# Rows of h for six of twelve chunks taken from PE through PSUM in place of DMA, with new scheduling targets

## The chip, the cores and the metric

The kernel runs on one core of a Trainium2 chip. A core has five engines that run side by side: PE (TensorE, matrix products into PSUM), DVE (VectorE), ACT (ScalarE), POOL (GpSimd) and SP, which here issues transfers. SBUF is the working memory of 128 partitions; PSUM, which PE writes and DVE and ACT read, has eight banks. Sixteen DMA engines carry out transfers. The metric is device time in microseconds (us); lower is better.

## The reference

A windowed attention feeds a gated feed-forward layer with a convolution along the sequence. The batch is 8, there are 8 heads of 64, the sequence is 576; the window is 32 to either side; d_model is 512, d_ff 1024, and the convolution has three taps.

```
scores = scale * (q @ k.T)            # masked outside the window, then softmax
x      = softmax(scores) @ v          # heads joined: (8, 576, 512)
h      = relu(x @ w_in)               # (8, 576, 1024)
conv   = sum_k conv_w[k] * h shifted by k - 1 along the sequence
out    = (h * sigmoid(conv)) @ w_out  # (8, 576, 512) float32
```

## The kernel before

**Tiling.** Attention runs by batch and by pair of heads: load q and k, cast to bf16, transpose on PE, scores on PE, exp on ACT, mask on DVE, values on PE, and the division by the row sums on DVE (`xn`). `xn` is transposed on PE into `xT`. The feed-forward part runs over twelve chunks of 384 rows of the sequence, three chunks for two batches (`ffn`, L942). For each of eight blocks m of 128 features, `first` (L747) multiplies by `w_in`, and a relu with factor 0.5 on ACT or DVE writes `hT`. Then come the convolution and the gate for four blocks at a time (`gates`, L856), and `second` (L912) multiplies the product `gT` by `w_out`. Chunk 1 is done in two halves of 192 columns; chunks 1, 4, 7 and 10 straddle two batches.

**The convolution and the turned rows.** The three taps are done on PE with 32x32 diagonal matrices (`diag_w`). To keep all sixteen 32x32 tiles of the array at work, rows 32r to 32r+31 of block m are written to the output partitions that begin at 32((r + m) mod 4):

```
to = 32 * ((r + m) % 4)
tensor.matmul(bank(ps, i)[to:to + 32, 0:n], diag_w[32 * r:32 * r + 32, kk, m, :], taps(m, kk, 32 * r, 32 * r + 32), ...)
```

So the convolution of block m comes out with its rows turned by 32 times (m mod 4). ACT takes the tanh of it (two instructions of two banks, into `tn`), and DVE forms (tanh + 1) times h, which needs h turned by the same amount; w_out's rows are loaded turned alike. For the first block of four the turn is nil and DVE reads h from `hT`. For the other three, `moves` (L822) issues DMAs on SP that copy h, with its rows turned, from `hT` into `gT` (two DMAs for each turn, since it wraps around), and the product then overwrites `gT` in place. The product is one instruction for block 0, one for block 1, and one for blocks 2 and 3 together.

**The order.** The kernel does not leave its order to a compiler. Each step is handed to a planner (`Order.add`, L42) with the engines that may do it, an estimate of its duration, what it reads and writes, the number of PSUM banks that it opens, and a target time. `Order.run` (L76) walks through a model of the engines: whenever an engine is free, it takes the ready step with the smallest target. The order that comes out is the order of the instructions in the program, and it is kept. Targets come from a formula (`PARAMS`) and are replaced by the entries of `TIMES`, one list for each kind of step. The names are `qk` and `v` for loads, `mv` for moves, `ph` for first products, `rl` for relus, `cv` for convolutions, `th` for tanh, `pr` for gate products, `py` for second products, and so on. The planner also sets dummy matmuls (`warm`) where it expects PE to be idle in the first 95 us.

All transfers but five go through SP's one queue in that order: loads of q, k, v and the weights, moves of h, and stores of the result. An instruction that waits there holds up what stands behind it.

The constant `GE`, the number of chunks whose rows are moved by DVE or ACT, is 0 here, so all twelve chunks use DMAs.

Of the kernel before, what the change touches and what calls it, by code (L numbers as in the profile page):

```python
# [16 lines left out]
GE = 0  # L17

# [196 lines left out]
def kernel(  # L215
# [98 lines left out]
    def two(kind):  # L314

        return kind[0], kind[1], "port"
# [391 lines left out]
    def x_turned(b, c, n):  # L708

        t, d = pair_t[b * NP + NP - 1]  # L710
        t = t + Q["XT"] * d + 0.1 * c + (Q["B0"] if b == 0 and c else 0.0)
# [110 lines left out]
    def moves(c, qds, part, t):  # L822
        kind, halves, n, taps, gate = views(c, part)
        for s_ in range(1, 4):
# [15 lines left out]
            if c < GE:  # L840
                continue
# [14 lines left out]
    def gates(c, qd, part, t, late):  # L856
# [27 lines left out]
        for m0, count, us in ((0, 1, (0,)), (1, 1, (0,)), (2, 2, (1,))):  # L884
            m = 4 * qd + m0
            ii = [("h", kind, m, p_) for p_ in halves] if m0 == 0 else [
                ("gm", c % 3, m + x, p_, to) for x in range(count) for p_ in halves for to in range(0, 128, 32)]

            def product(e, m=m, m0=m0, count=count):
                if count > 1:  # L890
                    vector.scalar_tensor_tensor(
                        out=gate(m, count=count), in0=tn[:, m0:m0 + count, 0:n], scalar=1.0,
                        in1=gate(m, count=count), op0=ALU.add, op1=ALU.mult)
                else:
                    vector.scalar_tensor_tensor(
                        out=gate(m), in0=tn[:, m0, 0:n].rearrange("p (i x) -> p i x", x=HW),
                        scalar=1.0, in1=gate(m) if m0 else taps(m, 1), op0=ALU.add, op1=ALU.mult)

            o.add("pr", {"DVE": two(dve(n * count))}, product, late,
                  reads=[("tn", tn_i, u) for u in us] + ii,  # L900
# [66 lines left out]
    for b in range(B):  # L967
# [48 lines left out]
    "wic": [0.16, 15.86, 10.72, -5.27, 20.24, 27.55, 66.33, 50.26],  # L1016
# [113 lines left out]
```

## Time and profile before

| | |
|---|---|
| time, median of three runs | 243.39 us (242.74 to 246.04) |
| time of the profiled execution | 244.45 us |
| its span, first to last instruction | 242.5 us |
| granted PE clock, mean | 0.965 |
| busy share of PE, DVE, ACT, POOL | 89%, 69%, 73%, 20% |
| moved by DMA | 49.63 MB in 67420 packets |

The profile is one execution, seen by the hardware profiler. Busy time is the time in which at least one instruction of the engine was under way. In rows of groups stand the line (L295, a helper that records every operation), the engine, the operation, what it writes and reads with the shapes, the count, and then busy us and the mean ns of one instruction, and the idle time of the engine ahead of it with what ended it. The matmuls overlap, so that their mean is longer than busy time divided by count. The granted clock is the share of full speed that PE was allowed. A chain of waits follows the work that ended last back to the start.

### The profile page before, as it was taken

The page shows a single profiled execution, that of the slowest core. Times are in us where ns is not written, and L with a number is a line of the kernel's source. Part 1 is how long each engine was busy: PE and PEld are TensorE (multiplying, and loading weights), DVE is VectorE, ACT ScalarE, POOL GpSimd, SP SyncE. Part 2 cuts the span into 40 slices and gives each one's busy share as a digit, 9 for nine tenths or more (in the row PEclk, how much of TensorE's full clock was granted, in tenths as well). Part 3 has the DMA queues.
Part 4 walks back from the last instruction along what each step waited for, and adds up shares of the span by engine and source line. Part 5 has one row for each costly group of instructions (what it writes and reads, how often), then busy time and mean ns, then how long its engine had stood idle before and what let it go on. Part 6 is the DMA issues. An engine that isn't in the chain of part 4 may idle for free.

```text
span 242.5 us, 9363 instructions
## 1 busy us (share of the span) xinstructions
PE 215.5 (89%) x4004; PEld 130.6 (54%) x4035; DVE 168.2 (69%) x313; ACT 176.8 (73%) x308; POOL 47.8 (20%) x60
## 2 busy tenths in 40 slices
PE   2788797579999859989999999999999999999993
PEld 1546684355655447556556455565556556554441
DVE  7264967965149796999689788989787697217530
ACT  2658788777699858867985898789495958567541
POOL 4414243211355340110433121112000000000000
PEclk9999999759999985999999999999999999999999
DMA  6999999989999898959979999955125033125334
GB/s 151 232 296 277 379 187 252 240 208 357 310 229 300 228 327 221 288 113 283 256 194 254 255 221 272 277 150 182 40 76 174 3 132 100 39 74 181 111 132 182
DMA packets 67420, 49.63 MB, mean 205 GB/s; under 512 B 46364, under 2 KB 52532, under 8 KB 67380
## 3 DMA queue, kind: packets, MB, share of 16 engines
q1 hardware_dynamic: 67024, 48.44, 74.1%
q10 hardware_dynamic: 356, 0.60, 1.1%
q8 instruction: 31, 0.51, 1.0%
q14 instruction: 9, 0.07, 0.1%
HBM read 32.52 MB, written 9.44 MB: 173 GB/s over the span
## 4 chain that ended last, share of the span: by engine, by line
PE 61%; DMA 21%; ACT 6%; issue 4%; DVE 3%; SPq 3%; POOL 1%; ACTq 0%; POOLq 0%
PE pst L295 61%; DMA vst<-in_v_dram 6%; DMA qst<-in_q_dram 5%; DMA kst<-in_k_dram 4%; DMA wst<-in_moe_w_out_dram 3%; SPq L295 3%; DMA out_dram<-wst 2%; ACT attn L295 2%; DVE xn L295 1%; ACT kT L295 1%; ACT qb L295 1%; ACT wst L295 1%; ACT tn L295 1%; ACT hT L295 1%; DVE xT L295 1%
## 5 line engine op out<-in xcount | busy, mean ns | idle before, releaser
L295 PE MATMUL pst<-xT,w_in_sb 128*128 128x385 bf16 (+3 forms) x448 | 72.5, 307 | 1.0 <-DVE xT L295 0.7
L295 PE MATMUL pst<-w_out_sb,gT 128*128 128x512 bf16 x261 | 63.7, 379 | 3.0 <-issue 0.9
L295 PEld LDWEIGHTS <-w_in_sb 128*128 128x128 bf16 x448 | 39.7, 98 | 23.5 <-issue 3.4
L295 PEld LDWEIGHTS <-gT 128*128 128x128 bf16 x288 | 27.2, 98 | 30.5 <-issue 1.3
L295 ACT ACTIVATE attn<-pst 128x640 bf16<-128x640 f32 (+1 forms) x64 | 39.2, 665 | 3.8 <-PE pst L295 3.7
L295 ACT ACTIVATE tn<-pst 128x768 f32<-128x768 f32 (+1 forms) x52 | 37.8, 760 | 5.8 <-PE pst L295 5.4
L295 DVE SCALAR_TENSOR_TENSOR gT<-tn,gT 128x384 bf16<-128x384 f32 (+2 forms) x52 | 37.3, 737 | 4.3 <-ACT tn L295 2.5
L295 ACT ACTIVATE hT<-pst 128x385 bf16<-128x385 f32 (+3 forms) x74 | 33.7, 460 | 9.1 <-PE pst L295 8.2
L295 ACT COPY wst<-pst 128x512 f32<-128x512 f32 x34 | 19.9, 585 | 24.5 <-PE pst L295 24.1
L295 DVE TENSOR_SCALAR hT<-pst 128x385 bf16<-128x385 f32 (+3 forms) x38 | 18.0, 478 | 21.9 <-PE pst L295 11.7
L295 DVE TENSOR_TENSOR attn<-attn,mask 128x1152 bf16<-128x1152 bf16 (+2 forms) x36 | 27.0, 764 | 7.2 <-ACT attn L295 6.9
L295 DVE TENSOR_TENSOR xn<-pst,rec 128x640 bf16<-128x640 f32 (+2 forms) x36 | 25.8, 737 | 0.4
L295 POOL CAST ve<-vst 128x512 bf16<-128x512 f32 x21 | 15.0, 722 | 37.9 <-DMA vst<-in_v_dram 29.4
L295 PE MATMUL pst<-hT,diag_w 32*32 32x384 bf16 (+1 forms) x1248 | 21.5, 321 | 1.1 <-ACT hT L295 0.6
L295 POOL CAST qb<-qst 128x1152 bf16<-128x1152 f32 (+1 forms) x13 | 14.3, 1100 | 39.4 <-DMA qst<-in_q_dram 23.1
L295 PE MATMUL pst<-qT,kT 64*128 64x64 bf16 x576 | 17.1, 197 | 4.2 <-ACT attn L295 1.7
L295 PEld LDWEIGHTS <-kT 64*128 64x128 bf16 x576 | 12.0, 98 | 13.0 <-issue 9.7
L295 PEld LDWEIGHTS <-attn 128*64 128x64 bf16 x640 | 13.1, 115 | 10.0 <-issue 5.2
L295 PEld LDWEIGHTS <-diag_w 32*32 32x32 bf16 x1248 | 12.5, 88 | 11.0 <-issue 8.1
L295 PE MATMUL pst<-ve,attn 128*64 128x65 bf16 x384 | 15.4, 200 | 3.1 <-ACT attn L295 1.5
L295 POOL CAST kb<-kst 128x1152 bf16<-128x1152 f32 (+1 forms) x10 | 11.0, 1099 | 22.5 <-DMA kst<-in_k_dram 19.5
L295 DVE SCALAR_TENSOR_TENSOR gT<-tn,hT 128x384 bf16<-128x384 f32 (+1 forms) x26 | 14.2, 545 | 1.5 <-ACT tn L295 1.5
(47 smaller groups left out, 207.1 us busy)
## 6 DMA issues: line engine op xcount, KB each, us to landing
out_dram<-wst SPq DMA_DIRECT2D x11, 768.0 KB, 4.0
qst<-in_q_dram SPq DMA_DIRECT2D x14, 576.0 KB, 7.8
kst<-in_k_dram SPq DMA_DIRECT2D x14, 576.0 KB, 6.9
vst<-in_v_dram SPq DMA_DIRECT2D x24, 256.0 KB, 6.3
vst<-in_v_dram SPq DMA_DIRECT2D x16, 192.0 KB, 8.3
wst<-in_moe_w_in_dram SPq DMA_DIRECT2D x2, 1024.0 KB, 7.5
gT<-hT SPq DMA_DIRECT2D x14, 144.0 KB, 3.7
gT<-hT SPq DMA_DIRECT2D x34, 48.0 KB, 4.0
```

The source lines that it names most:

```text
L295: return lambda *args, **kwargs: fixed(do(*args, **kwargs))
```

## The change

For chunks 0 to 5 (`GH` is 6) the moves are left out. In their place stands a step `hr` on PE behind each convolution: twelve 32x32 matmuls with an identity (`ident32`, which was there before) write h of blocks 1 to 3, turned, into three PSUM banks. DVE's products for these blocks read h from there instead of from `gT`. The product of blocks 2 and 3 becomes two instructions. For the planner, products that read PSUM do not use the port that DVE and POOL share. Chunks 6 to 11 are as before. Each target in `TIMES` is another number, there are 14 targets for `hr`, and `mv` has 27 in place of 51. A branch in `x_turned` that transposes by DMA is added for batches from `XB`, which is 9, on.

```
+GH = 6
+XB = 9
+XL = 1800.0
...
     def x_turned(b, c, n):
         t, d = pair_t[b * NP + NP - 1]
+        if b >= XB:
+            for i in range(n):
+                o.add("xd", {"SP": dma(512, 25, 1, XL)}, lambda e, i=i: sync.dma_start(
...
+                          transpose=True),
...
+            return
...
-            if c < GE:
+            if c < max(GE, GH):
                 continue
...
+        hp = Banks(3) if c < GH else None
+        if hp:
+            def again(e):
+                for m0 in (1, 2, 3):
+                    for r in range(4):
+                        to = 32 * ((r + m0) % 4)
+                        tensor.matmul(
+                            bank(hp, m0 - 1)[to:to + 32, 0:n], ident32[32 * r:32 * r + 32, :],
+                            taps(4 * qd + m0, 1, 32 * r, 32 * r + 32), start=True, stop=True,
+                        )
+            o.add("hr", {"PE": pe(n / 2.4 + 60.0, "conv")}, again, late - 0.5,
+                  reads=[("pc", c, qd, part)], writes=[("hr", c, qd, part)], opens=hp,
+                  claims=[("g", c % 3, m, p_) for m in ms[1:] for p_ in halves],
+                  sub=qd + 2 * int(c == 1 and part == 0))
-        for m0, count, us in ((0, 1, (0,)), (1, 1, (0,)), (2, 2, (1,))):
+        for m0, count, us in (
+            ((0, 1, (0,)), (1, 1, (0,)), (2, 1, (1,)), (3, 1, (1,))) if hp
+            else ((0, 1, (0,)), (1, 1, (0,)), (2, 2, (1,)))
+        ):
...
-                        scalar=1.0, in1=gate(m) if m0 else taps(m, 1), op0=ALU.add, op1=ALU.mult)
+                        scalar=1.0, in1=(
+                            taps(m, 1) if not m0 else gate(m) if not hp
+                            else bank(hp, m0 - 1)[:, 0:n].rearrange("p (i x) -> p i x", x=HW)
+                        ), op0=ALU.add, op1=ALU.mult)
-            o.add("pr", {"DVE": two(dve(n * count))}, product, late,
-                  reads=[("tn", tn_i, u) for u in us] + ii,
+            o.add("pr", {"DVE": dve(n * count) if hp and m0 else two(dve(n * count))}, product, late,
+                  reads=[("tn", tn_i, u) for u in us] + ii, ps=[hp] if hp and m0 else [],
...
 TIMES = {
...
+    "hr": [51.56, 44.36, 55.05, 40.86, 66.04, 57.58, 88.82, 87.48, 113.53, 111.1, 98.45, 122.43, 128.37,
+        103.87],
...
```

More of the change, by code (lines that the diff above doesn't have):

```diff
@@ L710, in x_turned @@
         t, d = pair_t[b * NP + NP - 1]
+        if b >= XB:
+            for i in range(n):
+                o.add("xd", {"SP": dma(512, 25, 1, XL)},
+                      lambda e, i=i: sync.dma_start(
+                          xT_pp[b // 2 % 2][:, :, b % 2, 128 * (c + i):min(S, 128 * (c + i) + 128)],
+                          xn_pp[b % 2][0:min(128, S - 128 * (c + i)), c + i, :, :].rearrange("p h d -> p (h d)"),
+                          transpose=True),
+                      t + Q["XT"] * d + 0.1 * (c + i), reads=[("xn", b % 2, i_, p_) for i_ in range(NP) for p_ in (0, 1)],
+                      writes=[("xT", b // 2 % 2, b % 2, c + i)], sub=c + i)
+            return
         t = t + Q["XT"] * d + 0.1 * c + (Q["B0"] if b == 0 and c else 0.0)
@@ L883, in gates @@
                   sub=qd + 2 * int(c == 1 and part == 0))
-        for m0, count, us in ((0, 1, (0,)), (1, 1, (0,)), (2, 2, (1,))):
+        hp = Banks(3) if c < GH else None
[16 more added lines that the diff above has]
+        ):
             m = 4 * qd + m0
-            ii = [("h", kind, m, p_) for p_ in halves] if m0 == 0 else [
+            ii = [("h", kind, m, p_) for p_ in halves] if m0 == 0 else [("hr", c, qd, part)] if hp else [
                 ("gm", c % 3, m + x, p_, to) for x in range(count) for p_ in halves for to in range(0, 128, 32)]
@@ L999 @@
 TIMES = {
[16 rows of a table removed]
-    "wic": [0.16, 15.86, 10.72, -5.27, 20.24, 27.55, 66.33, 50.26],
[36 rows of a table removed]
-    "woc": [92.89, 108.38, 80.47, 26.38, 74.95, 60.09, 73.65, 29.52],
[44 rows of a table removed]
[16 rows of a table added]
+    "wic": [9.77, -0.55, 23.61, 66.31, 22.41, 46.77, 25.62, 17.63],
[36 rows of a table added]
+    "woc": [40.32, 59.04, 39.76, 27.86, 36.19, 43.45, 41.37, 49.63],
[47 rows of a table added]
 }
```

193 rows, old and new, of the table TIMES are left out of this document.

## The prediction

> **What bounds the kernel now.** I read the page first: busy tenths, clock, DMA row, and the chain that ended last.
>
> ```profile
> PE   2788797579999859989999999999999999999993
> ...
> PEclk9999999759999985999999999999999999999999
> DMA  6999999989999898959979999955125033125334
> ...
> q1 hardware_dynamic: 67024, 48.44, 74.1%
> ...
> PE 61%; DMA 21%; ACT 6%; issue 4%; DVE 3%; SPq 3%; POOL 1%; ACTq 0%; POOLq 0%
> ```
>
> A slice is 242.5 / 40 = 6.06 us. The DMA engines are full for 26 slices, to about 160 us, and then nearly idle; PE has its holes and its lowered clock in the first 16. So there are two stages. The chain in order of time (start, us, what) shows the border, for after this piece it is PE almost alone:
>
> ```profile
> 149.60 3.48 PE pst L295 x95
> ```
>
> The windows view, cut there, gives the stages in numbers (stretch, length, then busy us of PE, PEld, DVE, ACT, POOL, the granted clock, the DMA share, GB/s); the fourth row is the same view for the dummy matmuls alone, which keep PE awake and compute nothing:
>
> ```profile
> 20.00:150.00 130.00, 115.06 (x2352) 74.41 (x2366) 99.84 (x177) 103.78 (x183) 38.02 (x41) 0.93 0.98 258
> 100.00:160.00 60.00, 57.43 (x1109) 34.05 (x1119) 52.97 (x87) 48.67 (x84) 12.94 (x13) 1.00 0.94 235
> 150.00:242.50 92.50, 87.66 (x1480) 48.81 (x1488) 57.64 (x98) 62.73 (x110) 3.22 (x4) 1.00 0.43 125
> ```
> ```profile
> 20.00:150.00 130.00, 4.41 (x9) 1.26 (x12) 0.00 (x0) 0.00 (x0) 0.93 0.98 258
> ```
>
> Stage one, 20 to 150: DMA 98% busy, PE 115.06 - 4.41 = 110.65 us of real work in 130. Stage two: PE 87.66 of 92.5, nothing else near its limit. Who waits in stage one, and for what, shows the waits view (us in total, times, longest), first for all engines from 20 to 150, then for the SP queue from 0 to 150:
>
> ```profile
> POOL ve L295 <- DMA vst<-in_v_dram: 22.3, 11, 7.2
> POOL kb L295 <- DMA kst<-in_k_dram: 19.0, 7, 6.8
> POOL qb L295 <- DMA qst<-in_q_dram: 19.0, 7, 4.8
> ...
> PE pst L295 <- ACT attn L295: 5.3, 10, 1.0
> ```
> ```profile
> SPq L295 <- ACT hT L295: 10.1, 5, 4.3
> SPq L295 <- DMA qst<-in_q_dram: 6.3, 6, 1.6
> ```
>
> POOL, which casts most loads, stands 60.3 us for loads: they are taken up the moment they land. And the SP queue, which issues loads and moves in one order, stands 10.1 us for a relu (hT), with loads queued behind the move that waits. Loads through a full DMA set stage one; PE sets stage two.
>
> **What is removed.** For chunks 0 to 5 the 48 moves of rows (gT<-hT). Their issues, the time to landing, who stood for them, and the sizes of the moves of all twelve chunks:
>
> ```profile
> L295 SPq DMA_DIRECT2D gT<-hT x48: 599/630/4715, 37.0 to 146.1; - x48
> ...
>   DMA gT<-hT: 0.9, 3
> ...
> DMA to landing us min/median/max: 3.0/4.0/8.0
> ```
> ```profile
> gT<-hT SPq DMA_DIRECT2D x14, 144.0 KB, 3.7
> gT<-hT SPq DMA_DIRECT2D x34, 48.0 KB, 4.0
> gT<-hT SPq DMA_DIRECT2D x20, 72.0 KB, 3.4
> gT<-hT SPq DMA_DIRECT2D x14, 96.0 KB, 2.3
> ...
> gT<-hT SPq DMA_DIRECT2D x20, 24.0 KB, 2.4
> ```
>
> The latency itself is worth next to nothing: 0.9 us were spent waiting for landings. What counts is load on DMA. The sizes sum to 6912 KB; each chunk has the same share, so six of them 3456 KB, 3.54 MB. Queue q1 spent 0.741 x 242.5 = 179.7 us on 48.44 MB: by bytes the moves cost 3.54 / 48.44 x 179.7 = 13.1 us. By packets (rows of 768 B: 768 in each of chunks 0, 2, 3, 5; rows of 384 B: 1536 in each of 1 and 4; 6144 of 67024) they cost 16.5 us. I take the middle, 14.8. On SP go 48 x 0.63 = 30 us of issuing and the 10.1 us of waiting, which I count only as what lets loads use the freed DMA time.
>
> **What is added on PE.** 14 groups of 12 matmuls through 32x32 tiles (ten of 384 columns, four of 192 for chunk 1's parts), right behind a convolution of the same shape and tile mode. The convolutions of these chunks, from the groups by form between 20 and 150, with the DVE rows needed next, and then the tanh row of the whole run:
>
> ```profile
> L295 DVE TENSOR_TENSOR xn<-pst,rec 128x640 bf16<-128x640 f32 x16 | 12.7, 815 | 0.2
> ...
> L295 DVE SCALAR_TENSOR_TENSOR gT<-tn,gT 128x768 bf16<-128x768 f32 x10 | 10.2, 1025 | 0.6 <-DMA gT<-hT 0.6
> ...
> L295 PE MATMUL pst<-hT,diag_w 32*32 32x384 bf16 x480 | 8.9, 332 | 1.1 <-ACT hT L295 0.6 <-ACT attn L295 0.4
> ...
> L295 DVE SCALAR_TENSOR_TENSOR gT<-tn,gT 128x384 bf16<-128x384 f32 x12 | 7.3, 612 | 0.3 <-ACT tn L295 0.3
> ...
> L295 PE MATMUL pst<-hT,diag_w 32*32 32x192 bf16 x192 | 2.8, 272 | 0.0
> ...
> L295 DVE SCALAR_TENSOR_TENSOR gT<-tn,gT 128x192 bf16<-128x192 f32 x4 | 1.3, 351 | 0.0
> ```
> ```profile
> L295 ACT ACTIVATE tn<-pst 128x768 f32<-128x768 f32 x44 | 33.9, 809 | 5.4 <-PE pst L295 5.1
> ```
>
> A full convolution is three rounds of 16 tiles: 8.9 / 10 / 3 = 0.297 us a round; a half one 2.8 / 4 / 3 = 0.233. A turning is one round with 12 tiles used: 10 x 0.297 + 4 x 0.233 = 3.9 us. Lower bound by the tiles used, three quarters: 2.9; upper bound, each standing alone for one matmul's length, 10 x 0.332 + 4 x 0.272 = 4.4. I take 3.9, since the tiles run side by side in the row. The products of blocks 1 to 3 now wait for the turning in place of a landing; it ends some 0.3 us after the convolution, and the first tanh, which they wait for anyway, runs 0.81 us (the tanh row): covered, and at worst 14 x 0.3 = 4.2 us of DVE's, with the exps' masks and xn queued behind.
>
> **What changes on DVE.** A full gate's double product (1025 ns) becomes two single ones (612): 10 x 0.199 = 2.0 us; in chunk 1 two of 351 for one of about 612 at 384 elements: 4 x 0.09 = 0.4. Reading PSUM instead of SBUF: from 612 at 384 and 1025 at 768 elements, 640 would take 887; the product that does read PSUM takes 815. So between -0.07 us and nothing for each of 42; I take nothing. Together 2.4 us, hidden: DVE would hold (99.84 + 2.4) / 119.7 = 0.85 of the shortened stage, and held 52.97 / 60 = 0.88 from 100 to 160. Without that cover it is 2.4 us.
>
> **What is held in PSUM.** Each turning takes three more of eight banks beside the convolution's four, until DVE has done its products. Queued behind on PE are the scores, first and second matmuls, which need one or two banks each. No trace of before shows seven banks held. Lower end nothing (a gain is excluded: banks only get fewer); upper end PE standing in all 14 gates for both tanh, 14 x 2 x 0.81 = 22.7 us. The nearest row is PE waiting for ACT to empty banks, 5.3 / 10 = 0.53 us each; I take one such wait in every other gate, 7 x 0.53 = 3.7 us. The Trainium skill, "TensorEngine Tiling (Array Packing)", section Performance Considerations, says that tiling speeds up TensorE but not the emptying of PSUM, which may become the bottleneck; by that rule the 3.7 would be nearer to the upper end.
>
> **New targets.** They reorder everything. The order's worth is not in the trace; I take nothing, with 4.8 us to either side, what PE leaves unused in stage two (92.5 - 87.66). The transposing DMA in x_turned costs nothing: it needs b of 9 or more, and b ends at 7. Chunks 6 to 11 keep their moves.
>
> **The sum.** Stage one has two caps. DMA: 130 x 0.98 - 14.8 = 112.6 us, at 0.98 busy 114.9 us. PE: 110.65 + 3.9 = 114.55 us, and the best it sustained beside a full DMA is 57.43 / 60 = 0.957, so 119.7 us. PE's is the later, and the gain 130 - 119.7 = 10.3 us. ACT would then be at 103.78 / 119.7 = 0.87, over its 0.81 from 100 to 160, so this is no small order. Less 3.7 for PSUM: 6.6 us net, none in stage two. The profiled execution took 244.45 us (span 242.5); 244.45 - 6.6 = 237.85. It lay 1.06 above the median of 243.39, so the forecast is 236.8 us, -2.7%.
>
> **Rivals.** First, PSUM becomes the bound and it ends slower. Its place: the seven banks between a convolution and the last product. Against a gain of 10.3 it decides from 10.3 / 14 = 0.74 us lost a gate, under one tanh; from 1.09 it is over 2% slower, and at the upper end, 1.62, the time is 243.39 - 10.3 + 22.7 = 255.8. For it: ACT and DVE, which empty the banks, are at 0.80 and 0.77 in stage one (103.78 and 99.84 of 130). Against: PE's waits for them are short now.
>
> Second, the relief is hidden: freed DMA time isn't used, since a load also waits for its staging tile (the 6.3 us row), and PE gains nothing. Then 243.4 with the turnings covered, 247.3 with 3.9 us uncovered. Against it: POOL's 60.3 us of standing for loads say that the tiles are free early.
>
> Third, it goes better, since the clock comes back:
>
> ```profile
> 40.00:60.00 20.00, 15.16 (x354) 9.68 (x357) 15.05 (x28) 14.96 (x24) 3.90 (x5) 0.74 0.97 262
> 90.00:100.00 10.00, 9.48 (x134) 7.08 (x134) 7.70 (x13) 8.16 (x16) 0.83 (x2) 0.67 0.97 241
> ```
>
> At full clock this work saves at most 0.26 x 15.16 + 0.33 x 9.48 = 7.1 us: 236.8 - 7.1 = 229.7. It needs PE fed without holes around 40 and 85 us. The Trainium skill, "TensorE: Matmul & The Clock Gate", section Why this matters for your kernels, asks for no idle gap over about 3 us; the rows above show the lowered clock but not what set it off.
>
> That the change doesn't do what it says is excluded for the moves: the test in the code is on c alone.
>
> **Numbers.** The forecast's case 0.46, of it 0.09 above 238.5; the clock 0.12; the hidden relief 0.22; PSUM 0.20. About 2% can be told from no change here: 238.5 and 248.3. Faster 0.37 + 0.12 = 0.49; within 0.09 + 0.22 = 0.31; slower 0.20. The range, 228 to 249, leaves out some 0.03 below and 0.17 above; it takes in the order's 4.8 about the forecast. As both signs weigh: the forecast's own range is 232 to 242.
>
> **What would show it.** The last v load was issued here (the SP queue's timeline):
>
> ```profile
> 161.57 0.54 SPq L295 DMA_DIRECT2D vst<-in_v_dram  x1
> ```
>
> Right: 48 moves fewer; that load about ten us earlier; PE over 0.92 of stage one; turnings of about 0.3 us; products of 0.61 us from PSUM. Wrong: the loads end as before; PE waiting on DVE's products or tanh, at least 10 us in all; or products longer than 0.8 us.

## The result and the profile after

| | before | after |
|---|---|---|
| time, median of 18 runs each, same chip | 243.52 us (241.73 to 248.38) | 248.68 us (244.34 to 251.47) |
| ratio, with its 95% interval | | 1.0123 (1.0074 to 1.0173) |
| profiled execution, and its span | 244.45, 242.5 | 249.70, 247.9 |
| granted PE clock, mean | 0.965 | 0.957 |
| packets and bytes of queue q1 | 67024, 48.44 MB | 60112, 44.90 MB |

The change made the kernel slower, by 1.2%, where 2.7% faster was forecast. The ratio takes in only the executions within 1.5% of each kernel's fastest, 15 of 18 before and 5 of 18 after, which is why it is smaller than that of the medians (1.021). The profiled execution of the changed kernel lies some 3 us above what the ratio gives, so a difference of that size between the times of the two traces means nothing by itself.

The page of the changed kernel, the same lines as before (busy tenths in 40 slices of 6.2 us, the clock, the DMA engines, queue q1, and the chain that ended last by engine):

```profile
PE   2788796679899678999999999999989999999993
...
PEclk9999998559999977999999999999999999999999
DMA  6999999999999799249978295053211443225254
...
q1 hardware_dynamic: 60112, 44.90, 65.7%
...
PE 76%; DVE 8%; DMA 5%; ACT 4%; issue 4%; SPq 1%; POOL 0%; ACTq 0%; DVEq 0%; POOLq 0%
```

DMA's share of the chain fell from 21% to 5%, and its row has gaps from slice 17 on, where it was nearly full up to slice 26 before. PE's share of the chain rose from 61% to 76%. In the chain in order of time, PE alone makes up two long pieces (start, us, what, count), and the first begins at 104.85, where the same kind of piece began at 149.60 before:

```profile
104.85 68.17 PE pst L298 x1353
...
181.66 62.53 PE pst L298 x950
```

The windows view, cut as before (PE, PEld, DVE, ACT, POOL, clock, DMA share, GB/s), and its row for the dummy matmuls alone:

```profile
20.00:150.00 130.00, 115.20 (x2454) 71.22 (x2452) 95.63 (x188) 97.82 (x175) 38.79 (x43) 0.92 0.88 241
100.00:160.00 60.00, 59.87 (x1217) 33.27 (x1214) 49.97 (x92) 46.74 (x82) 12.34 (x14) 1.00 0.62 165
150.00:248.00 98.00, 93.33 (x1567) 51.51 (x1564) 57.19 (x98) 67.82 (x119) 1.74 (x3) 0.99 0.34 105
```
```profile
20.00:150.00 130.00, 2.40 (x7) 0.68 (x7) 0.00 (x0) 0.00 (x0) 0.92 0.88 241
```

The freed DMA time is there: its share from 100 to 160 fell from 0.94 to 0.62, and PE is at work for 59.87 of these 60 us. But in 20 to 150 PE did 115.20 - 2.40 = 112.8 us of real work against 110.65 before, and the turnings are some 4 us of it. The two figures are not quite alike, since the trace of before lacks 27 records of second products; their weight loads, 288, are all in both traces. The rows of the whole run, before and after:

```profile
L295 PE MATMUL pst<-w_out_sb,gT 128*128 128x512 bf16 x261 | 63.7, 379 | 3.0 <-issue 0.9
```
```profile
L298 PE MATMUL pst<-w_out_sb,gT 128*128 128x512 bf16 x288 | 67.3, 380 | 0.1
```

Of the missing ones 12 fall into 20 to 150 and 15 behind it. By the busy time of the same products in the changed kernel they are worth some 1.6 and 2.0 us. So before did about 112.2 us in stage one: the changed kernel did as much, but 3.9 of it is turnings, and at 150 us it is some 3 us behind with the rest. It has 93.33 us of PE's work left where the kernel before had 87.66 + 2.0 = 89.7.

Who waited in stage one, first POOL from 20 to 150, then the SP queue from 0 to 150:

```profile
POOL ve L298 <- PE pst L298: 21.4, 3, 11.3
POOL ve L298 <- DMA vst<-in_v_dram: 21.1, 10, 6.4
POOL qb L298 <- PE pst L298: 15.1, 4, 6.0
...
POOL kb L298 <- PE pst L298: 6.1, 2, 4.5
...
POOL kb L298 <- DMA kst<-in_k_dram: 5.4, 5, 2.1
...
POOL qb L298 <- DMA qst<-in_q_dram: 1.6, 4, 0.5
```
```profile
SPq L298 <- ACT ve L298: 16.3, 6, 6.3
SPq L298 <- ACT wst L298: 11.8, 4, 6.3
SPq L298 <- ACT kb L298: 7.6, 3, 6.3
```

POOL stood 60.3 us for loads of q, k and v before, and 21.1 + 5.4 + 1.6 = 28.1 now; in exchange it stands 42.6 us for PE, that is for a buffer that PE still has to read. The SP queue stands 16.3 + 7.6 = 23.9 us for casts on ACT (`ve`, `kb`): a load can't be issued before its staging tile has been cast. In the row of `wst` it is nearly all stores of the result that wait for ACT's copy. The loads now run ahead of PE about as far as their tiles let them. The last v load was issued at 149.86, 11.7 us earlier than before, and nothing came of it:

```profile
149.86 0.44 SPq L298 DMA_DIRECT2D vst<-in_v_dram  x1
```

The added work itself, from the groups by form between 20 and 150 (mean ns of one behind the comma):

```profile
L298 DVE SCALAR_TENSOR_TENSOR gT<-tn,pst 128x384 bf16<-128x384 f32 x30 | 15.0, 546 | 1.8 <-PE pst L298 1.7
...
L298 PE MATMUL pst<-hT,ident 32*32 32x384 bf16 x120 | 3.9, 347 | 0.0
...
L298 DVE SCALAR_TENSOR_TENSOR gT<-tn,pst 128x192 bf16<-128x192 f32 x12 | 3.5, 349 | 2.9 <-PE pst L298 2.8
...
L298 PE MATMUL pst<-hT,ident 32*32 32x192 bf16 x48 | 1.2, 272 | 0.5 <-ACT tn L298 0.5
```

### The profile page after: what moved, and what is told of

It is laid out like the page before. It is cut to its first block, busy times and chain, and to the rows that moved or that the text cites. A ratio compares the mean times of both kernels' runs of the same rounds, so it can differ in the third digit from the quotient of the medians.

```text
span 247.9 us, 9646 instructions
## 1 busy us (share of the span) xinstructions
PE 221.3 (89%) x4198; PEld 130.2 (53%) x4198; DVE 163.5 (66%) x322; ACT 175.9 (71%) x311; POOL 47.8 (19%) x62
## 3 DMA queue, kind: packets, MB, share of 16 engines
q1 hardware_dynamic: 60112, 44.90, 65.7%
## 4 chain that ended last, share of the span: by engine, by line
PE 76%; DVE 8%; DMA 5%; ACT 4%; issue 4%; SPq 1%; POOL 0%; ACTq 0%; DVEq 0%; POOLq 0%
PE pst L298 76%; DMA kst<-in_k_dram 2%; ACT attn L298 2%; DVE xn L298 2%; DMA gT<-hT 1%; DVE gT L298 1%; DVE vo L298 1%; DMA qst<-in_q_dram 1%; DVE attn L298 1%; DVE hT L298 1%; DVE xT L298 1%; SPq L298 1%; ACT wst L298 0%; ACT ve L298 0%; DVE rec L298 0%
## 5 line engine op out<-in xcount | busy, mean ns | idle before, releaser
L298 PE MATMUL pst<-w_out_sb,gT 128*128 128x512 bf16 x288 | 67.3, 380 | 0.1
L298 ACT ACTIVATE hT<-pst 128x385 bf16<-128x385 f32 (+3 forms) x78 | 36.1, 469 | 14.7 <-PE pst L298 13.9
L298 ACT COPY wst<-pst 128x512 f32<-128x512 f32 x31 | 18.2, 586 | 21.8 <-PE pst L298 20.8
L298 DVE TENSOR_SCALAR hT<-pst 128x193 bf16<-128x193 f32 (+3 forms) x34 | 15.1, 456 | 17.3 <-PE pst L298 16.7
L298 DVE SCALAR_TENSOR_TENSOR gT<-tn,pst 128x384 bf16<-128x384 f32 (+1 forms) x42 | 18.5, 490 | 4.7 <-PE pst L298 4.5
L298 PEld LDWEIGHTS <-attn 128*64 128x64 bf16 x640 | 14.6, 123 | 12.5 <-issue 8.3
L298 DVE SCALAR_TENSOR_TENSOR gT<-tn,gT 128x384 bf16<-128x384 f32 (+1 forms) x24 | 17.6, 752 | 5.2 <-DMA gT<-hT 4.0
L298 PE MATMUL pst<-ve,attn 128*64 128x65 bf16 x384 | 17.6, 210 | 2.6 <-DVE xn L298 2.3
L298 POOL CAST qb<-qst 128x1152 bf16<-128x1152 f32 (+1 forms) x14 | 14.7, 1054 | 23.9 <-PE pst L298 15.1
L298 PE MATMUL pst<-vo,attn 128*64 128x65 bf16 x256 | 16.2, 212 | 2.4 <-DVE vo L298 2.4
L298 DVE COPY xT<-pst 128x1024 bf16<-128x1024 bf16 (+1 forms) x21 | 11.3, 555 | 9.5 <-PE pst L298 8.8
```

The lines of the kernel that those rows point to most:

```text
L298: return lambda *args, **kwargs: fixed(do(*args, **kwargs))
```

## The experiments

After the result the leading theory (A) was: PE and the order it is held to set the time; the moves were hidden, and the turnings add their PE time one for one. Its rivals: the banks held in PSUM cost the time; the new order costs it; or the loads do set stage one, and something took the gain back. Ratios are to the kernel before on the same chip, with 95% intervals; one hundredth is 2.4 us. The traces are one execution each.

### Relief alone: no_moves

The kernel before, in its own order, without the 48 moves; the products read `hT` unturned.

```diff
             def move(e, m=ms[0], s_=s_):
+                if c < 6:
+                    return
...
             def product(e, m=m, m0=m0, count=count):
-                if count > 1:
+                if c < 6 and m0:
+                    base = taps(m, 1)
...
+                    vector.scalar_tensor_tensor(out=o_, in0=t_, scalar=1.0, in1=src, op0=ALU.add, op1=ALU.mult)
+                elif count > 1:
```

> The kernel before in its own order, with the 48 moves of chunks 0 to 5 left out; the products read h from hT, unturned, so the output is not the reference's. The relief of the DMA engines alone, with nothing added. The prediction's reasoning (loads through a full DMA set the time up to 150 us) expects 10.3 us less, a ratio of about 0.96. The theory that PE is the limit from 100 us on and that its holes before that are not made by the moves expects 0.99 to 1.00.

Measured: 1.0097 (1.0052 to 1.0143); the medians are 245.44 and 244.42 us. All the DMA time that the change frees, with nothing put in its place, is worth no gain, where the prediction's reasoning asked for 10.3 us. The windows view from 100 to 150, in this run and in that of before:

```profile
100.00:150.00 50.00, 46.37 (x869) 26.99 (x875) 43.39 (x70) 39.19 (x68) 11.57 (x10) 1.00 0.70 188
```
```profile
100.00:150.00 50.00, 47.70 (x894) 27.85 (x900) 43.71 (x70) 40.52 (x69) 11.77 (x11) 1.00 0.94 237
```

DMA's share falls from 0.94 to 0.70, and PE is no busier. Why it comes out a little slower is not settled, but two things in its record can hide a gain of a us or two. The granted clock was lower, 0.965 in the mean of all 12 executions against 0.969 in 23 of before, whose medians differ by only 1.0 us. And in its trace PE stands 6.5 us from 20 to 150 for what the waits view calls "issue", against 2.3 in before (see the last section).

### The turnings: no_turn, turn_twice

The changed kernel in its order, with the turnings left out (its products read `hT` unturned), and with every turning done twice.

```diff
             def again(e):
+                return
...
-                            taps(m, 1) if not m0 else gate(m) if not hp
-                            else bank(hp, m0 - 1)[:, 0:n].rearrange("p (i x) -> p i x", x=HW)
+                            taps(m, 1) if not m0 or hp else gate(m)
```
```diff
-                for m0 in (1, 2, 3):
+                for m0 in (1, 2, 3, 1, 2, 3):
```

> The changed kernel in its own order, with the 168 turning matmuls left out; the products read h from hT, unturned, so the output is not the reference's. Theory A, PE's added work is the cost (4.2 us, all on PE's path): ratio to before 1.012 - 0.017 = 0.995. Theory B, the new order is the cost: stays at 1.01. Theory C, banks held until the products is the cost: 0.995 or lower, since the hold goes too, with fewer waits of PE on DVE.

> The changed kernel with each turning done twice, 168 matmuls more (and 336 instructions more on PE), banks held as before. Theory A: another 4.2 us, ratio 1.03. Theory B: unchanged, 1.012. Theory C: unchanged, 1.012, since nothing is held longer than by a third of a us. If PE's instruction blocks arriving late are a cost of their own, more than 1.03, with gaps inside dense groups of small matmuls.

Measured: 0.9959 (0.9912 to 1.0006) and 1.0299 (1.0217 to 1.0380). Zero, one and two turnings give 0.9959, 1.0123 and 1.0299: steps of 4.0 and 4.3 us, each known to within some 2 us. What one turning takes of PE shows the timeline, from its first matmul to the first of the next step, in chunk 1 of the changed kernel and then of turn_twice:

```profile
68.67 0.29 PE L298 MATMUL pst<-hT,ident 32*32 32x192 bf16 x12
68.89 1.90 PE L298 MATMUL pst<-w_out_sb,gT 128*128 128x512 bf16 x8
```
```profile
68.09 0.37 PE L298 MATMUL pst<-hT,ident 32*32 32x192 bf16 x24
68.39 1.90 PE L298 MATMUL pst<-w_out_sb,gT 128*128 128x512 bf16 x8
```

A single turning of 192 columns holds PE for 0.22 us and a double one for 0.30; those of 384 columns, read in the same way, take 0.30 and 0.46. So the first turnings are 10 x 0.30 + 4 x 0.22 = 3.9 us, which is the first step. The second pass adds only 10 x 0.16 + 4 x 0.08 = 2.0, less than the 4.2 that was expected of it, and the time rose by 4.3: at the least, none of it was covered.

In no_turn the planner still keeps the three banks apart until the products are done, but the products no longer read them, so no later step has to wait for them there. What the hold costs is read from the changed kernel itself: among the waits of PE's matmuls from 20 to 150 no row names the products (`DVE gT`).

### Early or late: early_x4, late_x3

The changed kernel with the turnings of chunks 0 and 1 done four times, or those of chunks 2 to 5 three times.

```diff
-                for m0 in (1, 2, 3):
+                for m0 in (1, 2, 3) * (4 if c < 2 else 1):
```
```diff
+                for m0 in (1, 2, 3) * (1 if c < 2 else 3):
```

> The changed kernel with the turnings of chunks 0 and 1 alone done four times (6 groups, 1.53 us for one pass by 0.297 and 0.233 us a group, so 4.6 us of PE work more, before 80 us). If PE's work costs its length wherever it stands: 1.012 + 0.019 = 1.031. If PE has slack before 100 us and is the limit only after: 1.012 to 1.018.

> The changed kernel with the turnings of chunks 2 to 5 alone done three times (8 groups, 2.38 us for one pass, so 4.8 us of PE work more, from 97 us on). If PE is the limit from 100 us on, by either theory: 1.012 + 0.020 = 1.032. If DMA or the other engines still set the time there: 1.012 to 1.02.

Measured: 1.0412 (1.0360 to 1.0465) and 1.0325 (1.0259 to 1.0391). The late work costs (0.0325 - 0.0123) x 244 = 4.9 us, the early work 7.1, each to within some 2 us. The first agrees with its expectation and the second is above it, but both expectations took a whole round of a convolution for each pass. By the timeline a turning of 384 columns takes 0.30, 0.65 and 0.81 us in one, three and four passes, and one of 192 columns 0.22 and 0.59 in one and four. So PE's work grew by only 8 x 0.35 = 2.8 us late and 2 x 0.51 + 4 x 0.37 = 2.5 early. Even before 80 us, with DMA full, PE's added time is not covered but costs more than itself. The traces show two companions: PE's standing for "issue" from 20 to 150 rose from 5.8 us to 7.9 (early), 8.0 (late) and 7.2 (turn_twice), and in early_x4 the granted clock was lower, 0.955 in the mean of its six executions against 0.962 in 18 of the changed kernel. How much of the surplus they make, these runs don't separate.

### Half of the change: new_targets_dma, old_targets

The new targets with all moves by DMA (`GH` = 0, targets for the moves made up), and the turned rows with the targets of before (those of the turnings made up: 0.5 ahead of the products).

```diff
-GH = 6
+GH = 0
...
+    "mv": [38.36, 38.36, 38.36, ...
```
```diff
-    "qk": [-6.1, 8.1, 10.67, -8.07, ...
+    "qk": [59.74, -55.85, -59.8, -25.67, ...
...
+    "hr": [22.63, 18.19, 16.49, 25.04, ...
```

> The new targets with the moves of all chunks by DMA as before (the 24 moves get targets 6 us ahead of those of the turnings that they replace). Theory A: 0.995 to 1.00, like before without the turnings' work. Theory B, the new order is bad by itself: 1.01 or more. The prediction's reasoning (DMA relief is worth 10 us): well slower than the changed kernel, 1.05.

> The changed kernel with the scheduling targets of the kernel before (the list of moves shortened by its first 24 entries, the targets of products repeated where one became two, each turning 0.5 ahead of its product). Only the turned rows are left of the change. Theory A (PE is the limit, the turnings' 4.2 us come on top, the moves were hidden): 1.017, so that the new targets of the change are worth about nothing to 1%; makeshift targets for the turnings may cost a little more, up to 1.03. The rival, that the new targets are what makes the changed kernel slower: 0.97 to 0.99 here.

Measured: 1.0612 (1.0529 to 1.0694) and 1.0527 (1.0476 to 1.0578); both are far outside what theory A allowed, and the first is near where the prediction's reasoning put it. Each half alone is worse than both together: an order fits the steps that it was set for. In the new order the moves do cost, 0.065 or 16 us against no_turn, so that they are hidden holds for the order that was set for them. How much of the two losses is the made-up targets, these runs can't tell. But the new targets by themselves are no cause of the slowdown: with them and without turnings, no_turn is no slower than the kernel before. Against no_moves, which has the old order and also does neither moves nor turnings in chunks 0 to 5, it is better by 0.0138, 3.4 us; in the traces PE stands 4.2 us less for "issue" there (2.3 against 6.5), so how much of it is the order stays open.

### DMA's room after 100 us: late_by_dma

The changed kernel with chunks 3 to 5 turned by DMA, each block's moves issued right after its relu.

```diff
+            if 3 <= c < 6 and m % 4:
+                kind_, halves_, n_, taps, gate = views(c, part)
+                for lo, to, cnt in turn(m % 4):
+                    sync.dma_start(gate(m, to, to + cnt), taps(m, 1, lo, lo + cnt))
...
             def again(e):
+                if c >= 3:
+                    return
...
-                            taps(m, 1) if not m0 else gate(m) if not hp
+                            taps(m, 1) if not m0 else gate(m) if not hp or c >= 3
```

> The changed kernel with its targets, but rows of h are turned by PE in chunks 0 to 2 alone; in chunks 3 to 5 each block's moves are issued as DMAs right after its relu, in the time from about 70 to 150 us, when DMA has room. PE has about 2.0 of the 4.2 us of turnings less. Theory A: 1.0123 - 0.008 = 1.004, if SP's 24 more issues (0.63 us each) delay no load that is needed. The rival, that the moves cost DMA time that loads need there: 1.02 or more.

Measured: 1.0457 (1.0400 to 1.0513). A miss for the theory as put, and the waits view shows why, in its rows for the SP queue and for POOL's casts from 20 to 150:

```profile
SPq L298 <- ACT hT L298: 12.0, 5, 9.4
```
```profile
POOL qb L298 <- DMA qst<-in_q_dram: 28.1, 11, 9.8
```

The edit issues 36 DMAs more (90 moves in the trace against 54), not the 24 of the expectation, and SP is at work on issues for 44.5 of the 50 us from 100 to 150 (27.5 in the changed kernel). It stands 12.0 us for relus, 9.4 in one wait, with loads queued behind; POOL's standing for q goes from 1.6 to 28.1 us, and PE is busy only 43.68 us from 100 to 150 (49.87 in the changed kernel). Here loads seem to come late enough to hold PE. That a DMA has room says nothing of the queue that issues to it.

### More moves: moves_twice

The kernel before with every move of chunks 0 to 5 issued a second time, into a spare tile.

```diff
+                if c < 6:
+                    t_ = spare[spare_n[0] % 7]
+                    spare_n[0] += 1
+                    for lo, to, cnt in turn(s_):
...
+                            sync.dma_start(t_[to:to + cnt, 0, 0:n].rearrange("p (i x) -> p i x", x=HW), taps(m, 1, lo, lo + cnt))
```

> The kernel before with each move of chunks 0 to 5 issued a second time, into a spare tile that nothing reads: 14.8 us of DMA time and 48 issues more, in SP's queue. If DMA sets the time to 150 us: 10 to 15 us more, 1.04 to 1.06. If PE sets it and DMA has just enough room: 1.00 to 1.02. Together with the run without the moves it shows on which side of the knee the kernel before lies.

Measured: 1.1213 (1.1151 to 1.1275), 29.6 us. Taking 48 moves away gained nothing, and adding 48 costs about the 30 us that SP needs to issue them. DMA's load is hardly what holds the kernel here, for DMA's share from 20 to 150 is lower than before, 0.86 against 0.98. Loads and moves come late out of the queue: DVE's products waited 12.2 us for moves up to 160 us, where before it was 0.9. The granted clock fell as well, to 0.928 in the mean of six executions against 0.969 of before, and what part of the 29.6 us goes with that was not separated. The kernel before lay near the point where the moves were still hidden.

### Do loads set stage one at all: no_v_loads, no_mask

The kernel before without the v loads from the third batch on; and without DVE's mask products in batches 1 to 4.

```diff
+            if b >= 2:
+                return
             lo = 128 * c - PAD
```
```diff
-              lambda e: vector.tensor_tensor(out=attn, in0=attn, in1=mask, op=ALU.mult),
+              lambda e: None if 4 <= g < 20 else vector.tensor_tensor(out=attn, in0=attn, in1=mask, op=ALU.mult),
```

> The kernel before without the loads of v from the third batch on; the casts of v stay and read what the tiles hold, so v is wrong there. About 36 us of DMA time are gone, and v never comes late. The prediction's reasoning (loads through a full DMA set stage one, PE could keep 0.957 there): stage one ends at the PE cap of 115.6 us, some 14 us earlier, ratio 0.94 to 0.95. Theory A (PE is fed well enough; the holes from 20 to 100 us are made by the chain of the attention and by the order, not by loads): 0.99 to 1.01.

> The kernel before without DVE's products with the mask for batches 1 to 4, so that scores outside the window count there. Some 13 us of DVE are gone and the chain from exp to values is shorter by that product; PE's work is unchanged. If PE's holes from 40 to 100 us are made by the chain of exp, mask and values on ACT and DVE: PE busier there and 0.98 or less. If PE is held by its own work and the order: 0.99 to 1.01.

Measured: 0.9911 (0.9875 to 0.9946) and 0.9886 (0.9830 to 0.9943): small gains, 2.2 and 2.8 us. The prediction's reading asked for 0.95 in the first.

### Both loads gone, and the mask too: no_v_no_moves, no_v_no_moves_no_mask

The edits of no_moves and no_v_loads together; then that of no_mask as well.

> The kernel before without the loads of v from the third batch on and without the 48 moves of chunks 0 to 5 (v and the rows of h are wrong there): some 51 us of DMA's 127 busy us of stage one are gone. Prediction's reading: 0.95 or less. Theory A: 0.985 to 1.00, as v alone gave 0.991 and the moves alone 1.01.

> The same, and without DVE's products with the mask in batches 1 to 4: some 51 us of DMA and 13 us of DVE are gone, PE's work is as before. If PE's own work in its fixed order is the limit: 0.975 to 0.99, about the sum of the single gains (0.991 and 0.989). If loads and the attention's chain hold PE in turn, each hiding the other: 0.96 or less.

Measured: 0.9939 (0.9890 to 0.9989) and 0.9900 (0.9842 to 0.9957). The windows view of no_v_no_moves, and behind it the two rows of before that have not been shown:

```profile
20.00:60.00 40.00, 33.05 (x729) 23.90 (x727) 31.19 (x64) 31.35 (x56) 13.95 (x17) 0.91 0.94 273
60.00:100.00 40.00, 35.08 (x750) 22.79 (x759) 27.07 (x45) 32.03 (x59) 12.70 (x14) 0.91 0.56 190
100.00:150.00 50.00, 48.76 (x965) 28.28 (x933) 43.42 (x73) 41.02 (x72) 11.53 (x9) 1.00 0.37 123
```
```profile
20.00:60.00 40.00, 32.25 (x730) 23.28 (x734) 29.83 (x63) 31.44 (x56) 12.05 (x16) 0.87 1.00 272
60.00:100.00 40.00, 35.12 (x732) 23.29 (x733) 26.30 (x46) 31.82 (x60) 14.20 (x15) 0.91 1.00 270
```

From 60 to 100 us DMA's share goes from 1.00 to 0.56 and PE's busy time from 35.12 to 35.08. What PE waits for in that stretch is nearly the same in both, and it is neither a load nor a cast on POOL; the two longest rows of no_v_no_moves and of before:

```profile
PE pst L295 <- issue: 2.1, 1, 2.1
PE pst L295 <- ACT attn L295: 1.5, 5, 0.6
```
```profile
PE pst L295 <- issue: 1.9, 3, 1.6
PE pst L295 <- ACT attn L295: 1.6, 5, 0.7
```

So PE's idle time there is not made by loads. The gains don't add up when the reliefs are joined, so loads and DVE's masks don't hide each other either.

### PE's work taken away: two_taps_early, two_taps_late

The kernel before with the third tap of the convolution left out in chunks 0 to 5, or in 6 to 11.

```diff
-            for kk in range(3):
+            taps_n = 2 if c < 6 else 3
+            for kk in range(taps_n):
...
-                            taps(m, kk, 32 * r, 32 * r + 32), start=(kk == 0), stop=(kk == 2),
+                            taps(m, kk, 32 * r, 32 * r + 32), start=(kk == 0), stop=(kk == taps_n - 1),
```

> The kernel before with the convolution's third tap left out in chunks 0 to 5: one round of 16 matmuls less in each of 14 gates, 10 x 0.297 + 4 x 0.233 = 3.9 us of PE's work, all of it before about 150 us; loads and moves are as before. If PE's work sets stage one (theory A): about 0.984. If the loads through a full DMA set it, as the prediction had it: 1.00. If the order's waits swallow part of it: between, 0.99.

> The kernel before with the third tap left out in chunks 6 to 11: 12 x 0.297 = 3.6 us of PE's work less, nearly all of it after 150 us, where both readings have PE as the limit: 0.985 by both. The measure for the early run: if this one gains and the early one does not, the early stage has another limit.

Measured: 0.9914 (0.9868 to 0.9959) and 0.9826 (0.9764 to 0.9887). By the timeline a convolution is shorter by 0.27 us without its third tap, so 3.2 us of matmuls less late, and 3.8 early. Late they give 4.3 us, early 2.1, between the two readings; both are known to within 1.5 us. PE's work counts in the early stage, but perhaps not alone.

### The instruction blocks: after_plus64

The changed kernel with 64 tiny matmuls ahead of everything. What it tests is told in the last section.

```diff
+    for _ in range(64):
+        tensor.matmul(pst[:, 7, 0:8], warm_sb[:, 0:128], warm_sb[:, 0:8], start=True, stop=True)
```

> The changed kernel with 64 tiny matmuls (8 columns) ahead of everything on PE, where PE is idle for its first us: 128 PE instructions more, no time of their own. They move the borders of PE's instruction blocks of 256 by half a block. If the stalls at those borders while DMA is full (5.5 us in the changed kernel's profile against 1.6 before) set the time: a change of 2 us or more to either side, likely down to 1.00. If they fall into slack: 1.012 as before, with the gaps at other places.

Measured: 1.0157 (1.0093 to 1.0221), the same as the change within the intervals.

## Why the prediction was wrong

**The step that failed: "Loads through a full DMA set stage one."** Both rows behind it were right as numbers and wrong as a limit. DMA was 98% busy with loads that came ahead of need, as the runs without them show; a transfer that comes early also fills the row. POOL's 60.3 us of standing for loads are idle time of an engine that was busy for only 38.02 of 130 us; nobody on the way to the end waited for it that long. The waits of PE itself would have said so: its longest row of before in stage one was for ACT, 5.3 us in ten pieces, and for a DMA it stood 0.2 us. The 21% of DMA in the chain were no price either: at 43.00 us the chain runs 6.74 us through a load of q, and PE stood 1.3 us for that load's cast. Taken away, the moves gained nothing (1.0097), and the moves with the v loads 0.6%, where the prediction's two caps called for over 5%.

**The two caps.** It follows that the move from 130 to 114.9 us on DMA was no gain, and that PE's 0.957, seen from 100 to 160, was no rate that stage one reaches when DMA is free. (The missing records lower it, too: 81 of 93 second products are recorded in those 60 us.) In fact from 100 us on PE did better than that after the change, 59.87 of 60. But from 20 to 100 us it did 65.33 - 2.40 = 62.9 us of real work in 80, against 67.37 - 4.41 = 63.0 before, and 1.8 of the 62.9 are turnings. DMA was still full there, and no_v_no_moves, where it was not, shows that PE does no more from 60 to 100 us when DMA is free.

**The moves' price.** 14.8 us of DMA and 30 us of SP were right as sizes, and the packets went down by 67024 - 60112 = 6912 (6144 were counted for the moves). The second issue of the moves points to SP's 30 us as a real cost where it isn't covered. In the kernel before it was covered.

**The turnings.** 3.9 us was predicted, 3.9 stands in the timeline, and 4.0 us come through in the time. The size agrees in part by luck: it was worked out for turnings that stand right behind a convolution of the same tile mode, and in the new order 13 of the 14 begin behind another kind of matmul. In the sum they were counted in PE's cap, where the gain from the relief paid for them; with no relief, they are wholly on the path.

**The products.** 612 ns from SBUF was taken for the read from PSUM; it was 546. The waits of products on the turning, 1.7 + 2.8 = 4.5 us of DVE in all, are near the 4.2 named as the worst case; the step of 4.0 us from no_turn, with 3.9 on PE, leaves little room for them.

**PSUM.** 3.7 us was taken, and nothing of it is seen: PE has no row of waiting for the products that empty the three banks, and it stood 0.5 us for a tanh, where the sign of "wrong" was 10 us. This rival, with a chance of 0.20, fell. The rule of the Trainium skill that spoke for it ("TensorEngine Tiling (Array Packing)", section Performance Considerations: tiling does not speed up the emptying of PSUM) did not bite here: PE's waits for DVE and ACT in stage one stayed short (us in total, times, longest):

```profile
PE pst L298 <- issue: 5.8, 5, 2.0
PE pst L298 <- DVE xn L298: 2.6, 3, 1.9
PE pst L298 <- DVE vo L298: 2.4, 2, 1.7
PE pst L298 <- ACT attn L298: 2.1, 3, 1.5
```

**The order.** Taken as nothing, with 4.8 us to either side; between the two kernels without moves and turnings it went with 3.4 us of gain. The 4.8 us that PE seemed to leave unused in stage two were in part the missing records, some 2.0 us.

**The sum as it came out**, in steps of runs: the moves away and the new order together, -1.0 us (no_turn), of which +2.4 stand in no_moves and -3.4 between the two; the turnings, +4.0 (no_turn to the change): +3.0, 1.2%. In the place of the gain of 10.3 us stands one of about 1.0, with an interval from 2.1 to nothing. The prediction's second rival had this: "the relief is hidden", with 247.3 us if the turnings are uncovered. Its reason, that a load also waits for its staging tile, stands in the trace of after as SP's 23.9 us of waits for casts. But it looks like the consequence, not the cause: the casts in turn stand for PE (POOL 42.6 us), so the tiles come free late because PE reads late.

**What was said to show it.** The moves were 48 fewer, the last v load came 11.7 us earlier, the turnings had the size named and the products were a little shorter than named: four of five signs of "right" came out, none of the three signs of "wrong" did, and the time still rose. Only the fifth, PE above 0.92 of stage one, failed: 115.20 of 130 is 0.886, dummies included. It was the one sign on the engine that sets the end; the others show that relief arrived, not that anyone needed it.

**What stays open.** What keeps PE at 35 of 40 us between 60 and 100, with the clock at 0.91: not the loads, and the mask products only in a small part. Of its 4.9 us of idle time in before, the rows name 1.9 for "issue" and 2.5 for ACT (exp 1.6, relu 0.6, tanh 0.3). Whether taking these away would gain their length, and how much the lowered clock adds, was not tested. Open, too, is why added matmuls cost about twice their own length.

## What to carry to other kernels

A resource that is 98% busy with work issued ahead of need is not a limit until its consumers on the critical engine wait for it; look first at what PE itself waits for, and test the reading by taking the load away before replacing it. In this kernel, whose order had been set for its parts, what was taken away gained a part of its time or none (moves 1.010, v loads 0.991, mask 0.989, an early tap 0.991; only a late tap gained all of it), while what was added to PE or to the issuing queue cost all of it or more (turnings 4.0 us, moves 29.6 us). So a trade of hidden DMA time for PE time can lose even where PE looks idle 15% of the stage.

## What the hardware showed that was not expected

**Stops of PE at even distances in its program.** In the changed kernel PE stands four times for nothing that the waits explain. The chain in order of time has them as "issue":

```profile
41.77 0.63 issue
...
49.46 1.33 issue
...
61.64 1.54 issue
...
91.74 2.03 issue
```

One of them falls into a convolution, which the timeline shows cut in two, 40 and 8 matmuls:

```profile
61.06 0.59 PE L298 MATMUL pst<-hT,diag_w 32*32 32x192 bf16 x40
63.19 0.28 PE L298 MATMUL pst<-hT,diag_w 32*32 32x192 bf16 x8 [1.54 <-issue]
```

Counted in PE's records (weight loads and matmuls), the stops lie ahead of numbers 1215, 1471, 1983 and 3007, so 256, 512 and 1024 apart. Ahead of each of the four the trace has a packet of 16 KB on instruction queue q8, whose 33 packets fit PE's 8396 records at 256 each, and PE goes on 1.3 to 1.5 us after it has landed (the one shown lands at 61.86, and PE goes on at 63.19). The Trainium skill, "Runtime: NRT & Kernel Launch", section Instruction fetch mechanics, says that instructions come in blocks of 16 KiB, 256 of them, and that crossing into the next is mostly hidden; the distances agree with the blocks, but up to 2.03 us were not hidden. After 100 us, with DMA at 0.62, no such stop of over 0.3 us stands in this chain, which suggests that a full DMA makes the block late; but in no_v_no_moves, with DMA at 0.56 from 60 to 100, one of 2.1 us is left at 86.4, and in turn_twice one of 1.4 us ends at 119.5. What makes them late is open.

In the changed kernel they cost little. With 64 tiny matmuls ahead of everything the borders fall half a block elsewhere, and the row of 5.8 us of "issue", the largest of PE's waits from 20 to 150 in the changed kernel (shown with PSUM above), has shrunk to 2.0. In after_plus64 the largest is:

```profile
PE pst L298 <- ACT attn L298: 3.4, 5, 1.5
```

The time stayed the same within the intervals, 1.0157 against 1.0123, and PE stood longer for ACT instead (exp 3.4 us against 2.1, tanh 2.1 against 0.5). So the stops seem to have stood where PE would have waited anyway. In other runs they may cost: no_moves and the runs with added turnings have more of them, and no run takes them away there.

**The clock from run to run.** The mean granted clock differs between executions of one and the same kernel, and the time with it: of no_moves' twelve, one took 243.45 us at 0.976 and one 248.19 at 0.957. Among the 23 executions of before that were taken beside these, a straight line gives 1.9 us for a hundredth of the clock; among 23 on another chip, beside the runs with two taps, 0.8. In those, the mean clock of all executions was 0.961 in two_taps_early, 0.967 in before and 0.974 in two_taps_late. By the two slopes that is an estimate of 0.5 to 1 us that hides a part of the early gain, and of 0.6 to 1.5 that makes the late one look larger. So small differences between kernels should be read together with their clocks; that the clock makes the difference was not tested.
